# Two-layer cached attention with a token mixer: the K of the unit between the layers moved behind the last V of the unit at the change

## The chip, the cores and the metric

The kernel runs on one core of a Trainium2 chip. The metric is the device time of one execution in microseconds (us); the median of three runs is compared. In this text MB is a million bytes and GB/s a billion bytes a second.

## The reference

Two kinds of layer alternate, twice each: attention over a long cache for one new token, and a mixer.

```
h = layernorm(x)                                   # x: (2, 1, 512)
q = h @ wq                                         # 32 query heads of 128, 8 K/V heads
s = q . k_cache / sqrt(128)                        # 2 x 8 K/V heads, 32768 keys of 128 each
x = x + (softmax(s) . v_cache) @ wo
h = layernorm(x)
x = x + w2 . gelu(w1 * h + b1) + b2                # per channel, 1792 hidden values
```

All data are f32. One cache (K or V of one batch row and one head) is 16.8 MB, and there are 32 of them, read once in each of the two layers: some 1,061 MB cross the DMA queue, and this is nearly all the kernel does.

## The kernel before, in words

**Units.** The work is cut into 32 units (layer, batch row, K/V head). A unit has 8 chunks of K and 8 of V, 2.10 MB each (a `[128, 4096]` f32 tile). A K chunk takes 8 products on TensorE (line L481, 512 keys each; the trace counts each product as two MATMUL rows, so a chunk is x16), a V chunk likewise (L638). When all 8 K chunks of a unit are through, `max_1`, `max_2`, `turn_scores` and `exponentials` make the weights of its softmax, in two halves `S[0]` and `S[1]` of four chunks, and only then can its V chunks be multiplied. So the V of a unit comes after the K of the next one, normally.

**The units around the changes of layer.** Batch row 0 goes over to the second layer while batch row 1 is still in the first. With the numbers of the code: unit 12 is (layer 0, row 0, head 5), unit 13 = `N1` is (0, 0, 7) and ends row 0's first layer, unit 14 is (0, 1, 5), the unit "between the layers", and unit 15 is (1, 0, 7), the first of the second layer. The same happens for row 1 with units 16 = `N2`, 17 and 18. After the last V of unit 13 comes row 0's mixer (`mix_1`, `take_rows`, `mix_2`, `hidden_sum` with 14 hidden tiles, `mix_3`, `to_columns`), and from that the query of unit 15 (`q_products`, `make_q`).

**Memory.** SBUF holds 13.6 cells of one chunk each; loads go to cells 0 to 10, the other places hold weights. Head 7 is used by both layers in neighbouring units, so part of its K and V stays: K chunks 0, 1, 2 in cells 0, 1, 2 (`KEPT_K`) and V chunks 1, 2, 3, 5, 6, 7 and most of 4 (`KEPT`; chunk 4 lies in cell 13 and in the first part of cell 6). Between unit 13's V and unit 15's V only cells 6 and 7 are free for everything that passes; there the loads are half chunks (`[128, 2048]`, 1.05 MB), which rotate through the four half cells.

**Order.** Everything is planned in Python before the first instruction: `stream` is the list of loads, sorted by a key, and counts time in chunks; `at(time, f, ...)` books every other step at such a time (`kend`, `vend`: the chunk times when the unit's K and V are through); a load's cell is picked by `spread`, which takes the cell with the best `fit`. All cache loads are issued by one engine (SyncE, line L189) in the stream's order, through one queue. A load waits until the old contents of its cell have been used, and everything behind it waits too.

**The fold.** After unit 12 its result rows are added to x: `out_2` (4 products into `rows`, line L296), then `fold_rows`, which copies `rows` to cell 13 (DVE, L710) and turns it there (TensorE, L699). Both are booked at `vend + 2` of unit 12, two chunks after its last V. The load of unit 13's V chunk 4 into cell 13 has to wait for that.

```
    def fold_rows():
        y = mem[:, (WCELL0 + WCELLS) * CK :][:, :D]
        nc.vector.tensor_copy(y, rows)
        fold(y, 0, B)
```

Of the kernel before, what the change touches and what calls it, by code (L numbers as in the profile page):

```python
# [41 lines left out]
DIRECT = 2  # L42
TAIL_GROUPS = (3, 3, 3, 2, 1)
IDLE = (4, 1, 3, 2)
KEEP_UP = 3
EPS = 1e-5


@with_exitstack
def gqa_mixer_kernel(ctx: ExitStack, tc: tile.TileContext, x, kt, v, wqo, cols, out):  # L50
# [21 lines left out]
    NCH = kt.shape[1] // (CK * DH)  # L72
# [5 lines left out]
    NU = LAYERS * U  # L78
    NT = NCH * JT
    HALVES = NCH // PACK  # L80
# [24 lines left out]
    WCELL0, WCELLS = RING * RING, 4  # L105
# [129 lines left out]
    booked, closed = {}, {}  # L235
# [110 lines left out]
    def row_tile():  # L346

        return S[HALVES - 1]
# [450 lines left out]
    def last_mixer(n):  # L799
# [21 lines left out]
        for k in range(2):  # L821
# [14 lines left out]
        for g in range(NG):  # L836
# [7 lines left out]
            )  # L844
        idle_products(IDLE[1])

# [99 lines left out]
    def parts(n, with_v):  # L946

        m = n + with_v
        if m < N1 or n > N3 and m > N3 + 1:

            loads = ((0, 4), (4, 2), (6, 2)) if m == NU else ((0, 2), (2, 2), (4, 2), (6, 2)) if m == N3 + 2 else GROUPS
            return [(c, k, NCH) for c, k in loads]
        if not with_v:
            loads = ((0, 3), (3, 1), (4, 2), (6, 2)) if n in (N1, N2) else ((0, 2), (2, 2), (4, 2), (6, 2))
            if n in (N1 + 1, N2 + 1):
                loads = ((0, 2), *((c, 1) for c in range(2, NCH)))
            if n in (N1 + 2, N3):
                loads = [(c, 1) for c in range(NCH)]
        elif n in (N1, N2):
            loads = ((0, 1), (1, 3), (4, 1), (5, 2), (7, 1))  # L960
        elif n in (N1 + 1, N2 + 1):
            loads = [(c, 1) for c in range(NCH)]
        elif n < N1:
            loads = ((0, 2), (2, 2), (4, 2), (6, 2))
        else:
            loads = [(c, 1) for c in range(NCH)]
        return [(c, k, RING) for c, k in loads]

    stream = []
    for n in range(NU):  # L970
        stream += [(n * NCH + c + m - 1, 0, n, c, m, limit) for c, m, limit in parts(n, 0)]
        for i, (c, m, limit) in enumerate(parts(n, 1)):
            if n in (N1, N2):
                key = (n + 1) * NCH + 1 + (i + 1) / (2 * NCH)
            elif n in (N1 + 1, N2 + 1):
                key = (n + 1) * NCH - 0.5 + max(c / (2 * NCH) - 0.5, c - 2 + m)
            elif n - N1 in FOLLOWS:
                key = (n + 1) * NCH + FOLLOWS[n - N1][c]
            else:
                key = (n + 1) * NCH + c + m - 1 + (LAG if N1 - 1 <= n <= N3 else 0)  # L980
            stream.append((key, 1, n, c, m, limit))
# [3 lines left out]
    kbeg, k_done, vbeg, v_done, vend_of, v_from, v_to, brings, starts, t = {}, {}, {}, {}, {}, {}, {}, [], [], 0  # L985
# [13 lines left out]
    def at(time, f, *a, rank=1):  # L999
        done.setdefault(time, []).append((rank, f, a))  # L1000
# [3 lines left out]
    mixed = {}  # L1004
    for n in range(NU):
        layer, b, h = unit_of(n)
        kend, vend = k_done[n, NCH - 1], vend_of[n]
        ahead = vend_of[n - 1] if n else 0
        urgent = n in (N1, N2, NU - 1)
        if n:  # L1010
            if n in (N1 + 2, N2 + 2):
                q2 = mixed[layer - 1, b] + 0.5
                q3 = q2 + 1
                place = S[1]
            else:
                place = S[0] if n in (N2 + 1, N3 + 1) else None
                q0 = kbeg[n] - (10 if n == N3 + 1 else 4 if n == N3 + 2 else 6)
                q1, q2, q3 = q0 + 1, q0 + 2, q0 + 2
            assert q3 <= kbeg[n]
            if n not in (N1 + 2, N2 + 2):  # L1020
                apart = not N1 <= n <= N3 + 2 and h not in opens
                if apart and layer == 1:
                    at(kbeg[n] - 11, make_q, n, 4)
                    at(q0, make_q, n, 5)
                    at(q1, make_q, n, 6)
                else:
                    at(kbeg[n] - (11 if apart else 9) if apart or n == N1 - 1 else q0, make_q, n, 0)
# [15 lines left out]
        if n in (N1 + 1, N2 + 1):  # L1043
            for k in range(2, 2 * (NCH - 3)):
                at(kend - 0.5 * k - 0.5, idle_products, KEEP_UP, rank=3)
            at(kend - 0.5, turn_scores, n, 0, rank=2)
            at(kend, q_products, n + 1, 0)
            at(kend, max_1, n)
            at(kend, max_2, n)
            at(kend, q_products, n + 1, 1)  # L1050
            for k in range(HALVES):
                at(kend, exponentials_at_once, n, 0, k, HALVES)
            at(kend + 0.5, q_products, n + 1, 2, 3)
            t1 = kend + 2
            assert mixed[units[n - 1][:2]] == kend == kbeg[n + 1] - 2
            at(t1, turn_scores, n, 1, rank=2)
            at(t1, exponentials_at_once, n, 1, rank=2)
            at(t1 + 1, sums, n)
            assert t1 + 1 < v_done[n, HC] - 1
        else:  # L1060
            t1 = max(kend + 2, ahead + (2 if urgent else 4))
            e = kend if N1 < n <= N3 else kend + 2
            soon = n in (N1 + 2, N3)
            assert not soon or e == kend and vbeg[n] == kend
            at(max(kend, e - 1), max_1, n, rank=int(not soon))
            at(e, max_2, n, rank=int(not soon))
            t0 = max(k_done[n, HC - 1], *(v_done[n - 1, c] for c in range(HC) if n), 0)
            if n in (N2, N3):
                t0 = max(t0, kbeg[n + 1] - (7 if n == N3 else 3))
            at(t0, turn_scores, n, 0)  # L1070
            if soon:
                assert t0 < e and v_from[n] % HALVES == 1
                for k in range(HALVES):
                    at(e, exponentials_at_once, n, 0, HALVES - 1 - k, HALVES, rank=0)
                at(e + 1, sums, n, 1)
            else:
                at(e, exponentials, n, 0)
            if n == NU - 1:
                t1 = ahead
                assert t1 >= kend + 2 and vbeg[n] == ahead  # L1080
            at(t1, turn_scores, n, 1)
            at(t1, exponentials, n, 1)
        at(t1 + (1 if n == NU - 1 else 2), denominators, n)
        if n == NU - 1:
# [2 lines left out]
            at(vend, last_out, n)  # L1087
            at(vend, last_mixer, n)
            continue
        assert vbeg[n + 1] >= vend and (n + 2 >= NU or vbeg[n + 1] > vend)  # L1090
        change = n in (N1, N2)
        at(vend if change else min(vend + 1, vbeg[n + 1]), out_0, n)
        at(vend + 0.5 if change else min(vend + 1, vbeg[n + 1]), out_1, n)
# [6 lines left out]
            at(vend + 2, fold_rows)  # L1100
        if units[n] == lay[layer, b][-1]:
            key = (layer, b)
            at(vend - 1 if change else vend, mix_1, key)
            at(vend + (1 if change else 2), take_rows, key, row_tile())
            at(vend + (1.5 if change else 3), mix_2, key)
            at(vend + (0 if change else 1), gelu_table)
            if change:

                assert k_done[n + 1, NCH - 1] == vend + 6
                at(vend + 1.5, hidden_sum, key)  # L1110
                at(vend + 4.5, highest, n + 1, 0)
# [32 lines left out]
    first = next(t for t, (*_, n, _, m, limit) in zip(starts, stream) if n > N3 and m == PACK)  # L1144
    for k in range(0, NCH, PACK):
        book(k, 2 * PACK, first + k)
    closed[WCELL0] = closed[WCELL0 + 1] = kbeg[N2 + 1]
    closed[WCELL0 - 1] = kbeg[N3 + 2] - 8
    first_input()
    for step in range(4):  # L1150
# [90 lines left out]
```

## Time and profile before

| | |
|---|---|
| device time, three runs | 2488.03, 2488.17 (median), 2489.24 us |
| span of the profiled execution, first to last instruction | 2486.6 us |
| what the median has around that span | 1.6 us |
| TensorE busy | 1413.2 us, 57% |
| packets of the load queue | 99.2% of the time of 16 DMA engines |
| mean granted TensorE clock | 0.777 |

The profiled execution's device time is not listed apart from the three runs; its span is what the rows below are counted in, and the 1.6 us is taken as constant. A row of the chain or of the timeline gives start, duration, engine, line, and what was written from what; "idle before" tells what ended the wait. A row of the windows gives, for a stretch of time, the busy time of PE, PEld, DVE, ACT and POOL, then the granted clock, the DMA engines' busy share and the GB/s moved.

### The profile page before, as it was taken

To read this page: it belongs to the slowest core of one execution; us is meant where nothing else is said; L and a number is where in the kernel's file an instruction comes from. 1 tells how busy PE (TensorE), PEld (TensorE's weight loads), DVE (VectorE), ACT (ScalarE), POOL (GpSimd) and SP (SyncE) were. 2 spreads that over 40 slices of the span, in tenths; PEclk is the share of its full clock that TensorE was granted. 3 is DMA by queue.
4 is the path that set the end of the run, shared out by engine and by line. 5 is a ranking of instruction groups with operands and counts; after the bars stand their busy time and mean duration, and the time that the engine had idled before them with its cause. 6 is when DMAs were issued, how large, how long until landed. Compare 5 with 4: busy or idle time off the path is not lost.

```text
span 2486.6 us, 20856 instructions
## 1 busy us (share of the span) xinstructions
PE 1413.2 (57%) x9438; PEld 386.1 (16%) x9438; DVE 256.6 (10%) x659; ACT 185.5 (7%) x544; POOL 4.9 (0%) x17
## 2 busy tenths in 40 slices
PE   4544545556555454657677675455555664456546
PEld 1111111111111111112122121111111111111112
DVE  1000000000000000003113110000000000010002
ACT  0000000000000000002012000000000000011002
POOL 0000000000000000000000000000000000000000
PEclk8777777776777777888888887777677777777878
DMA  9999999999999999999999999999999999999996
GB/s 421 434 433 429 433 437 430 434 436 431 427 435 431 436 427 432 431 429 412 431 433 415 429 432 432 434 435 430 436 429 429 429 435 434 428 436 431 434 435 287
DMA packets 30594, 1062.54 MB, mean 427 GB/s; under 512 B 3749, under 2 KB 3753, under 8 KB 4394
## 3 DMA queue, kind: packets, MB, share of 16 engines
q1 hardware_dynamic: 30216, 1061.17, 99.2%
q8 instruction: 74, 1.21, 0.2%
q14 instruction: 14, 0.11, 0.0%
q10 hardware_dynamic: 290, 0.04, 0.0%
HBM read 1061.19 MB, written 0.00 MB: 427 GB/s over the span
## 4 chain that ended last, share of the span: by engine, by line
DMA 72%; PE 26%; DVE 0%; issue 0%; another core or an unknown queue 0%; ACT 0%; SPq 0%; ACTq 0%
DMA mem<-in_v_dram 61%; PE acc L638 20%; DMA mem<-in_kt_dram 10%; PE scores L481 3%; DMA mem<-in_wqo_dram 2%; PE kept L162 1%; PE kept L395 1%; PE small L669 0%; PE small L510 0%; PE bcast L395 0%; PE small L797 0%; PE small L504 0%; PE kept L296 0%; PE kept L849 0%
## 5 line engine op out<-in xcount | busy, mean ns | idle before, releaser
L481 PE MATMUL scores<-mem,small_sb 128*32 128x512 f32 x4096 | 615.7, 724 | 544.5 <-DMA mem<-in_kt_dram 544.4
L638 PE MATMUL acc<-mem,S 128*16 128x512 f32 x4088 | 621.3, 737 | 473.0 <-DMA mem<-in_v_dram 471.3
L481 PEld LDWEIGHTS scores<-mem,small_sb 128*32 128x32 f32 x4096 | 147.2, 127 | 914.6 <-issue 839.2
L521 ACT ACTIVATE S<-S,small_sb 128x128 f32<-128x128 f32 x232 | 119.3, 518 | 1974.6 <-DVE small_sb L512 1377.0
L638 PEld LDWEIGHTS acc<-mem,S 128*16 128x16 f32 x4088 | 132.6, 110 | 839.6 <-issue 699.1
L496 DVE TENSOR_REDUCE small_sb<-scores 128x1 f32<-128x512 f32 x64 | 44.3, 692 | 743.8 <-PE scores L481 743.8
L516 DVE STREAM_TRANSPOSE S<-scores 128x512 f32<-128x512 f32 x64 | 45.5, 710 | 141.4 <-PE acc L638 137.2
L395 PE MATMUL kept<-mem,small_sb 128*2 128x512 f32 x96 | 54.5, 691 | 3.9 <-DMA mem<-in_wqo_dram 2.1
L296 PE MATMUL kept<-mem,small_sb 128*1 128x512 f32 (+1 forms) x236 | 42.1, 597 | 2.7 <-ACT mem L892 2.4
L521 ACT ACTIVATION_READ_ACCUMULATOR S<-S,small_sb 128x1 f32 x232 | 43.3, 187 | 0.0
L506 DVE TENSOR_REDUCE small_sb<-small 1x4 f32<-1x128 f32 x32 | 8.9, 279 | 294.1 <-PE small L504 294.1
L671 DVE RECIPROCAL small_sb<-small 128x4 f32<-128x4 f32 x32 | 5.9, 185 | 321.6 <-PE small L669 321.6
L680 DVE TENSOR_TENSOR small_sb<-small,small_sb 128x4 f32<-128x4 f32 x31 | 5.1, 164 | 299.1 <-PE small L678 299.1
L608 DVE SCALAR_TENSOR_TENSOR S<-acc,small_sb,S 128x128 f32<-128x128 f32 x93 | 32.6, 351 | 3.3
L892 ACT ACTIVATE S<-bcast,small_sb 128x512 f32<-128x512 f32 x28 | 21.6, 778 | 89.9 <-DVE small_sb L761 87.8
L606 DVE TENSOR_SCALAR S<-acc,small_sb 128x128 f32<-128x128 f32 x31 | 10.8, 350 | 146.7 <-PE acc L638 146.7
L162 PE MATMUL kept<-mem,small_sb 48*2 48x512 f32 x32 | 25.2, 929 | 0.0
L421 PE MATMUL small<-small_sb,mem 2*128 2x2 f32 x112 | 14.7, 248 | 17.9 <-DVE mem L417 17.9
L395 PE MATMUL bcast<-mem,small_sb 128*1 128x512 f32 (+1 forms) x40 | 20.9, 640 | 0.0
L678 PEld LDWEIGHTS small<-small_sb,S 128*128 128x128 f32 x62 | 13.2, 266 | 48.7 <-issue 41.9
L797 PE MATMUL small<-small_sb 128*128 128x128 f32 x120 | 18.7, 290 | 0.0
L504 PE MATMUL small<-small_sb 128*1 128x128 f32 x64 | 16.7, 354 | 3.3 <-DVE small_sb L502 3.3
(154 smaller groups left out, 340.9 us busy)
## 6 DMA issues: line engine op xcount, KB each, us to landing
mem<-in_kt_dram SPq DMA_DIRECT2D x14, 4096.0 KB
mem<-in_v_dram SPq DMA_DIRECT2D x11, 4096.0 KB
mem<-in_v_dram SPq DMA_DIRECT2D x13, 2048.0 KB
mem<-in_kt_dram SPq DMA_DIRECT2D x12, 2048.0 KB
mem<-in_kt_dram SPq DMA_DIRECT2D x24, 1024.0 KB
mem<-in_v_dram SPq DMA_DIRECT2D x21, 1024.0 KB
mem<-in_wqo_dram SPq DMA_DIRECT2D x4, 3840.0 KB
mem<-in_wqo_dram SPq DMA_DIRECT2D x3, 4096.0 KB
```

What stands on the lines that cost most here:

```text
L162: nc.tensor.matmul(q_ps[n][:B, :], low[:, j * B : (j + 1) * B], lowered[h][:, j * D : (j + 1) * D], start=(j == 0), stop=False,)
L296: nc.tensor.matmul((rows if to is None else to)[32 * g : 32 * g + b + 1, :], weights if b else weights[:, 1:], row, start=to is not None, ...
L395: nc.tensor.matmul(q_ps[n][:m, :], xnT[:, d, b : b + m], wq_at(h, d), start=(d == 0 and h not in lowered), stop=(d == last),)
L481: nc.tensor.matmul(sc_ps[n, half][32 * g : 32 * g + 32, :], q, kc[k * NG + g], start=(i == 0 and k == 0), stop=(i == PACK - 1 and k == SUB ...
L496: nc.vector.tensor_reduce(mx[n][:, half : half + 1], sc_ps[n, half], axis=AX.X, op=ALU.max)
L504: nc.tensor.matmul(pm[:1, :P], mxa, ident, start=True, stop=True)
L516: nc.vector.transpose(S[half], sc_ps[n, half])
L521: nc.scalar.activation(s[:, :, h], s[:, :, h], AF.Exp, bias=neg[n][:, h : h + 1], scale=SCALE, accum_out=lsum[n][:, half, h : h + 1],)
L608: nc.vector.scalar_tensor_tensor(t, acc[:, k * DH : (k + 1) * DH], mask[:, k : k + 1], t, op0=ALU.mult, op1=ALU.add)
L638: nc.tensor.matmul(acc[32 * g : 32 * g + R * QT, :], S[half][:, col : col + R * QT], vc[q], start=(c == v_from[n] and q < NG), stop=(c == ...
L797: nc.tensor.matmul(p[:, :P], ident, ident, start=True, stop=True)
L892: nc.scalar.activation(hid[key, f], px[key], AF.Gelu_apprx_tanh, bias=shift[key][:, f : f + 1], scale=slope[key][:, f : f + 1],)
```

## The change

Three keys of `stream` and the steps booked by them are changed, at both changes of layer (units 13 to 15 and 16 to 18):

- The first two K chunks of unit 14 came as one load ahead of unit 13's V. Now all eight come behind unit 13's last V, each as two half chunks.
- Unit 15's K chunks 0 and 1, which are resident, are now multiplied before unit 14's first V, and not among its V chunks; unit 15's query is made two chunks of K earlier than the end of unit 14's K. Unit 14's softmax steps move behind that.
- V chunks 5 and 6 of unit 13 are two loads, not one. V chunks 2, 3 and 4 of unit 14 are now loaded whole and no longer in halves.
- `idle_products` (10 products on data that nobody reads) are added around the last two V chunks of unit 13.
- Unit 12's `out_2` and `fold_rows` keep their times, `vend + 2`. Unit 13's softmax is booked earlier by one or two chunks.

```
+BETWEEN = (1.1, 1.2, 1.3, 2.1, 2.2, 3.1, 4.1, 5.1)
...
             if n in (N1 + 1, N2 + 1):
-                loads = ((0, 2), *((c, 1) for c in range(2, NCH)))
+                loads = [(c, 1) for c in range(NCH)]
...
         elif n in (N1, N2):
-            loads = ((0, 1), (1, 3), (4, 1), (5, 2), (7, 1))
+            loads = ((0, 1), (1, 3), (4, 1), (5, 1), (6, 1), (7, 1))
...
-        stream += [(n * NCH + c + m - 1, 0, n, c, m, limit) for c, m, limit in parts(n, 0)]
+        late = 0.5 if n in (N1 + 1, N2 + 1) else 0
+        stream += [(n * NCH + c + m - 1 + late, 0, n, c, m, limit) for c, m, limit in parts(n, 0)]
...
             if n in (N1, N2):
-                key = (n + 1) * NCH + 1 + (i + 1) / (2 * NCH)
+                key = (n + 1) * NCH + (i + 1) / (2 * NCH)
             elif n in (N1 + 1, N2 + 1):
-                key = (n + 1) * NCH - 0.5 + max(c / (2 * NCH) - 0.5, c - 2 + m)
+                key = (n + 1) * NCH + BETWEEN[c]
...
+                if n in (N1 + 1, N2 + 1):
+                    q0 = k_done[n - 1, NCH - 1] - 6
...
-            at(kend, q_products, n + 1, 0)
-            at(kend, max_1, n)
-            at(kend, max_2, n)
-            at(kend, q_products, n + 1, 1)
+            at(kend + 0.5, max_1, n)
+            at(kend + 1, max_2, n)
             for k in range(HALVES):
-                at(kend, exponentials_at_once, n, 0, k, HALVES)
-            at(kend + 0.5, q_products, n + 1, 2, 3)
+                at(kend + 1, exponentials_at_once, n, 0, k, HALVES)
...
-            t1 = max(kend + 2, ahead + (2 if urgent else 4))
-            e = kend if N1 < n <= N3 else kend + 2
+            t1 = max(kend + 2, ahead + (0 if n == N1 else 2 if urgent else 4))
+            e = kend if N1 < n <= N3 else kend + (1 if n == N1 else 2)
...
-        assert vbeg[n + 1] >= vend and (n + 2 >= NU or vbeg[n + 1] > vend)
+        assert vbeg[n + 1] >= vend and (n + 2 >= NU or vbeg[n + 1] > vend or n == N1 - 1)
...
-            at(vend - 1 if change else vend, mix_1, key)
+            at(vend - 2 if change else vend, mix_1, key)
+            if change:
+                for k in (2, 1):
+                    at(vend - k, idle_products, BEFORE, rank=2)
...
-                assert k_done[n + 1, NCH - 1] == vend + 6
+                assert k_done[n + 1, NCH - 1] == vend + 8
...
-    closed[WCELL0] = closed[WCELL0 + 1] = kbeg[N2 + 1]
+    closed[WCELL0] = closed[WCELL0 + 1] = k_done[N2, NCH - 1]
```

The load queue at the first change (SyncE), from the last V of unit 12 on. The width 2048 is a half chunk, 4096 a chunk, 12288 three chunks, 2560 and 1536 the two parts of unit 13's V chunk 4; the brackets name the semaphores waited for. Before:

```order
L189 DMA mem<-in_v_dram 128x8192 [waits DMAHW3_49,PE_49]
L189 DMA mem<-in_kt_dram 128x8192 [waits DMAHW5_49,DMAHW0_49,PE_49]
L189 DMA mem<-in_v_dram 128x4096 [waits DMAHW6_49,PE_49]
L189 DMA mem<-in_v_dram 128x12288 [waits DMAHW4_49,PE_49]
L189 DMA mem<-in_v_dram 128x2560 [waits DVE_49,PE_49,Pool_49]
L189 DMA mem<-in_v_dram 128x1536 [waits DMAHW7_49]
```

and with the change:

```order
L191 DMA mem<-in_v_dram 128x8192 [waits DMAHW5_49,PE_49]
L191 DMA mem<-in_v_dram 128x4096 [waits DMAHW0_49]
L191 DMA mem<-in_v_dram 128x12288 [waits DMAHW4_49,DMAHW2_49]
L191 DMA mem<-in_v_dram 128x2560 [waits DVE_49,PE_49,Pool_49]
L191 DMA mem<-in_v_dram 128x1536 [waits DMAHW6_49]
```

The 4.19 MB of unit 14's first K are gone from between unit 12's and unit 13's V. The load that waits for DVE and PE (width 2560) goes to cell 13 and stands directly behind the three-chunk load in both. In the built program its DVE wait is for the copy of `fold_rows` and its PE wait for the fold's last product. The cells differ, too: unit 13's last K load goes to cells 5 and 6 (7 and 8 before) and unit 12's last V load to cells 3 and 4 (5 and 6 before), so that the latter waits for V chunks 4 and 5 of unit 12 where it waited for chunks 2 and 3.

TensorE at the same place, from unit 13's last two K chunks on (`scores_2360` is unit 13's score tile, `scores_2440` unit 14's, `S0` and `S1` the weights, `kept2` the tile `rows`). Before:

```order
L481 MATMUL scores_2360<-mem_68,small_sb_66 32x512 x16
L638 MATMUL acc_83<-mem_68,S1_91 16x512 x8
L504 MATMUL small_92<-small_sb_66 1x128
L638 MATMUL acc_83<-mem_68,S1_91 16x512 x8
L510 MATMUL small_92<-small_sb_66 128x4
L481 MATMUL scores_2440<-mem_68,small_sb_66 32x512 x8
L678 MATMUL small_92<-small_sb_66,S1_91 128x4
L481 MATMUL scores_2440<-mem_68,small_sb_66 32x512 x8
L296 MATMUL kept2_87<-mem_68,small_sb_66 1x512 x4
L699 MATMUL small_92<-small_sb_66,mem_68 128x2 x4
L638 MATMUL acc_83<-mem_68,S0_90 16x512 x16
```

and with the change:

```order
L483 MATMUL scores_2360<-mem_68,small_sb_66 32x512 x16
L506 MATMUL small_92<-small_sb_66 1x128
L640 MATMUL acc_83<-mem_68,S1_91 16x512 x8
L512 MATMUL small_92<-small_sb_66 128x4
L640 MATMUL acc_83<-mem_68,S1_91 16x512 x8
L680 MATMUL small_92<-small_sb_66,S1_91 128x4
L640 MATMUL acc_83<-mem_68,S0_90 16x512 x16
L298 MATMUL kept2_87<-mem_68,small_sb_66 1x512 x4
L701 MATMUL small_92<-small_sb_66,mem_68 128x2 x4
```

The fold (kept2, then the small products of L699, now L701) stood behind unit 14's first two K chunks and ahead of unit 13's V. Now unit 13's V chunks 0 and 1 (the x16 on `S0`) stand ahead of it, and chunk 1 is part of the three-chunk load.

TensorE at the end of unit 14's K (`scores_2638` before, `scores_2652` now), where unit 15's scores begin (`scores_2749`, now `scores_2731`). Before:

```order
L481 MATMUL scores_2638<-mem_68,small_sb_66 32x512 x4
L395 MATMUL bcast_88<-mem_68,small_sb_66 1x512
L504 MATMUL small_92<-small_sb_66 1x128
L510 MATMUL small_92<-small_sb_66 128x4
L395 MATMUL bcast_88<-mem_68,small_sb_66 1x512
L638 MATMUL acc_83<-mem_68,S0_90 16x512 x4
```

and with the change:

```order
L483 MATMUL scores_2652<-mem_68,small_sb_66 32x512 x4
L483 MATMUL scores_2731<-mem_68,small_sb_66 32x512 x4
L506 MATMUL small_92<-small_sb_66 1x128
L483 MATMUL scores_2731<-mem_68,small_sb_66 32x512 x4
L512 MATMUL small_92<-small_sb_66 128x4
L483 MATMUL scores_2731<-mem_68,small_sb_66 32x512 x8
L640 MATMUL acc_83<-mem_68,S0_90 16x512 x16
```

The maximum of unit 14's scores (L504, L510) had the products of unit 15's query (bcast) between its steps; now it has unit 15's two resident chunks, 16 products, between the last K and the first V.

More of the change, by code (lines that the diff above doesn't have):

```diff
@@ L44 @@
 IDLE = (4, 1, 3, 2)
+BETWEEN = (1.1, 1.2, 1.3, 2.1, 2.2, 3.1, 4.1, 5.1)
 KEEP_UP = 3
+BEFORE = 5
 EPS = 1e-5
@@ L1045, in gqa_mixer_kernel @@
                 at(kend - 0.5 * k - 0.5, idle_products, KEEP_UP, rank=3)
+            q = mixed[units[n - 1][:2]]
+            assert q + 2 == kend == kbeg[n + 1]
+            at(q, q_products, n + 1, 0, 1)
+            at(q + 0.5, q_products, n + 1, 2, 3)
             at(kend - 0.5, turn_scores, n, 0, rank=2)
-            at(kend, q_products, n + 1, 0)
-            at(kend, max_1, n)
-            at(kend, max_2, n)
-            at(kend, q_products, n + 1, 1)
+            at(kend + 0.5, max_1, n)
+            at(kend + 1, max_2, n)
             for k in range(HALVES):
-                at(kend, exponentials_at_once, n, 0, k, HALVES)
-            at(kend + 0.5, q_products, n + 1, 2, 3)
+                at(kend + 1, exponentials_at_once, n, 0, k, HALVES)
             t1 = kend + 2
-            assert mixed[units[n - 1][:2]] == kend == kbeg[n + 1] - 2
             at(t1, turn_scores, n, 1, rank=2)
@@ L1068, in gqa_mixer_kernel @@
             if n in (N2, N3):
-                t0 = max(t0, kbeg[n + 1] - (7 if n == N3 else 3))
+                t0 = max(t0, kbeg[n + 1] - 7 if n == N3 else kend - 3)
             at(t0, turn_scores, n, 0)
```

## The prediction, made before the changed kernel was run

> **What bounds the kernel now.** I read the page first, for what is busy all the time.
>
> ```profile
> span 2486.6 us, 20856 instructions
> PE 1413.2 (57%) x9438; PEld 386.1 (16%) x9438; DVE 256.6 (10%) x659; ACT 185.5 (7%) x544; POOL 4.9 (0%) x17
> ...
> DMA  9999999999999999999999999999999999999996
> GB/s 421 434 433 429 433 437 430 434 436 431 427 435 431 436 427 432 431 429 412 431 433 415 429 432 432 434 435 430 436 429 429 429 435 434 428 436 431 434 435 287
> ...
> q1 hardware_dynamic: 30216, 1061.17, 99.2%
> ```
>
> The load queue never rests: its packets fill 99.2% of the span on all 16 DMA engines, while TensorE is busy for 57%. So the time is the bytes over the rate, plus every moment in which the queue is dry. TensorE's work counts only where it makes the queue dry, by keeping a cell from the next load. Apart from the first and the last, the only slices under 420 are 412 and 415, and those hold the two changes of layer (a slice is 62.2 us: 1119 to 1181 and 1306 to 1368). The windows there, cut where the load of unit 13's (16's) V ends and where the half chunks of the next unit's K end:
>
> ```profile
> 1100.00:1139.50 39.50, 21.61 (x144) 5.81 (x148) 5.16 (x13) 5.74 (x18) 0.00 (x0) 0.78 1.00 429
> 1139.50:1170.70 31.20, 28.33 (x201) 11.33 (x194) 15.61 (x28) 12.87 (x17) 0.54 (x1) 0.95 0.99 401
> 1170.70:1195.80 25.10, 20.74 (x157) 5.99 (x156) 8.23 (x20) 1.38 (x3) 0.54 (x1) 1.00 1.01 421
> ...
> 1327.90:1358.10 30.20, 26.58 (x194) 10.76 (x186) 15.24 (x28) 12.87 (x17) 0.54 (x1) 0.96 1.01 415
> 1358.10:1383.20 25.10, 21.39 (x166) 6.43 (x158) 8.47 (x20) 1.38 (x3) 0.54 (x1) 1.00 1.02 422
> ```
>
> The last column is GB/s. With half chunks and nothing late the queue moves 421 to 422, with larger pieces 429. Against 421, the stretch of unit 14's K at 401 lost (1 - 401/421) x 31.2 = 1.5 us, and the second one (1 - 415/422) x 30.2 = 0.5 us. These 2.0 us are all that the change can win at these places; the whole kernel has little else to give.
>
> **The first change of layer: the fold.** What can be lost is seen in the waits of the load queue's engine and in the chain at the same place.
>
> ```profile
> SPq L189 <- PE small L699: 23.1, 1, 23.1
> ```
> ```profile
> 1073.94 5.36 PE acc L638 x32
> ...
> 1079.32 23.64 DMA mem<-in_kt_dram
> ...
> 1103.09 3.64 PE scores L481 x16
> 1106.73 0.52 PE small L678 x2
> 1107.25 2.39 PE scores L481 x16
> 1109.64 0.91 PE kept L296 x8
> 1110.55 0.02 issue
> 1110.58 0.70 DVE mem L710
> 1111.28 0.04 issue
> 1111.33 1.07 PE small L699 x8
> ...
> 1112.44 0.33 SPq L189
> ```
>
> For 23.1 us the issuing engine stands at one load, that of unit 13's V chunk 4 into cell 13, until the fold is out of that cell. Nothing is issued meanwhile. In the kernel before this costs nothing: TensorE can do the fold once unit 14's first K chunks have landed (1103.09), and behind them the queue still holds unit 13's V chunks 0 to 3, 8.4 MB. The fold is done at 1112.4, and the three-chunk load is used only from 1122.45:
>
> ```profile
> 1083.56 5.34 PE L481 MATMUL scores<-mem,small_sb 128*32 128x512 f32 x32 [4.30 <-DMA mem<-in_kt_dram]
> ...
> 1122.45 3.34 PE L638 MATMUL acc<-mem,S 128*16 128x512 f32 x16 [8.24 <-DMA mem<-in_v_dram]
> ...
> 1144.38 1.91 PE L638 MATMUL acc<-mem,S 128*16 128x512 f32 x16
> ```
>
> In the order of the changed kernel TensorE has unit 13's V chunks 0 and 1 ahead of the fold, and chunk 1 is the first of the three-chunk load, which has one completion. So the fold waits for the whole of that load; and the load for cell 13, the next in the queue, waits for the fold. Behind the three-chunk load nothing is issued. The queue must run dry there, and stays so for the sum of
>
> - TensorE's chunk 1 after an idle wait: 3.34 us, the same instructions at 1122.45 in the kernel before, which also come cold out of a wait (warm they take 1.91, which I keep as the lower end);
> - `out_2`, the copy, the turning, the issue: from 1109.64 to 1112.44, 2.80 us;
> - the fixed time F of a load on an empty queue, from issue to first use beyond its bytes.
>
> F stands in no single row, so I bound it.
>
> ```profile
> 0.74 0.39 SPq L129 DMA_DIRECT2D mem<-in_wqo_dram  x1
> ...
> 32.50 7.76 PE L481 MATMUL scores<-mem,small_sb 128*32 128x512 f32 x52 [7.12 <-DMA mem<-in_kt_dram]
> ```
> ```profile
> 1368.11 6.82 DMA mem<-in_v_dram
> 1374.92 0.04 issue
> 1374.97 1.05 PE acc L638 x8
> ```
>
> At the kernel's start two loads, 4.19 and 8.39 MB, go out at 0.74 and are used at 32.50; at 429 GB/s 12.58 MB take 29.3, which leaves 2.4 us. In the stretch of half chunks a load went from issue to use in 6.82 us; its own 1.05 MB take 2.5 at 421, and part of the other 4.3 was a queue that still held something. So F is 2.4 to 4.3. I take 4.3: it is the row from the middle of the same stream, where the 16 DMA engines do not run in step, while the start has them all idle together. The dry time is then 3.34 + 2.80 + 4.3 = **10.4 us**; with the low ends, 1.91 + 2.80 + 2.4 = 7.1. The Trainium skill ("DMA: Bandwidth & Descriptors", the section on the anatomy of one DMA) puts the fixed cost of one DMA at about 2.0 us, fitted on DMAs that GpSimd issues; by that figure the dry time would be an estimated 8.1 and the total 2.3 us less than mine. The trace, with 2.4 at its lowest, lies a little above it.
>
> **The other edits.**
>
> - *Unit 12's last V load* now waits for TensorE's V chunks 4 and 5 (cells 3 and 4), and is issued at 1079.3, when the row at 1073.94 ends; in the queue ahead of it is only the end of unit 13's last K, used from 1083.56. That is 4.24 us from issue to use, against F = 4.3: 0.1 us dry, at most 0.1 by these bounds, and nothing if F is smaller. The two loads behind it wait for nothing late.
> - *Unit 14's K*: its first four half chunks are now in the queue before unit 13's V is finished, as before four others were; but unit 13's chunks 5, 6 and 7 are three loads, so when the last lands TensorE has one chunk left and not three. In the kernel before, two chunks (6.25 us for the pair at the low clock) and then the last chunk's 1.91 stood there. I count the 2.0 us as won.
> - *Sizes of pieces*: per change, 4.19 MB go from large pieces to half chunks (at 421 instead of 429, +0.2 us), 6.29 MB from half chunks to whole ones (-0.3). Both changes together: -0.2.
> - *Mixer, query and unit 14's softmax*: the mixer's work is the same. Its length against the eight chunks of K behind which it must hide is read from these rows.
>
> ```profile
> 1146.36 0.35 DVE L606 TENSOR_SCALAR S<-acc,small_sb 128x128 f32<-128x128 f32 x1 [17.10 <-PE acc L638]
> ...
> 1168.29 1.12 PE L917 MATMUL bcast<-S,small_sb 128*128 128x512 f32 x2 [0.36 <-DVE S L909]
> ...
> 1182.44 0.16 DVE L429 COPY small_sb<-small 128x4 f32<-128x4 f32 x1 [2.77 <-PE small L421]
> ```
>
> From `out_0` to `mix_3` it takes 21.9 us, to the ready query 36.2 (with unit 14's softmax steps in between). Sixteen half chunks take 16 x 2.5 = 40 us, so the query is there when unit 15's resident chunks are due, with some 4 us over. Those chunks, 2 x 1.9 us of products, hide the maximum and the exponentials of unit 14, which in the kernel before had the query's products. The loads that wait for them still have at least one or two half chunks ahead. I cost this at nothing; if the cover is gone, each change loses what the query is late.
> - *The extra idle products* lie in TensorE's waits for V chunks 6 and 7: nothing. Unit 13's softmax is booked earlier, and TensorE needs nothing of it that isn't due long before the three-chunk load has landed: nothing.
> - *The second change of layer* has no fold: `fold_rows` is called once, after unit 12. The load into cell 13 there finds a free place, and the queue holds over 20 MB worth of issued or issuable loads behind it. Nothing is lost.
>
> **The sum**, in the span: +10.4 + 0.1 - 2.0 - 0.2 = **+8.3**, so 2494.9; with the 1.6 us that the median has around this span, **2496.5 us**, or 0.33% slower. What can be told from no change is 0.2%, or 5.0 us: 2483.2 to 2493.1.
>
> **The rivals.**
>
> *The dry queue doesn't come, and only the gain stays.* It ends on the other side, if TensorE's chunk 1 needs to wait only for its own third of the three-chunk load. Then it starts two chunks, 4.19 MB or 9.8 us, earlier, 0.6 of the 10.4 us stay, and the sum is +0.6 + 0.1 - 2.2 = -1.5: 2486.7 us. For it: in the kernel before the same 23.1 us wait is free. Against it: the row at 1122.45 shows TensorE waiting 8.24 us for this load, and only then going through chunks 1, 2 and 3. It decides where the fold's wait ends: 10 us before the three-chunk load has landed it would be free.
>
> *The fixed time and the cold clock are at their low ends*: 7.1 - 2.2 = +4.9, or 2493.1. This is the lower edge of the first case, at which slower turns into no change.
>
> *The K of unit 14 runs into a new wait.* Its 16 half chunks have four half cells, and TensorE must take each within the three that are in flight, some 7 us. If the mixer's query is late for the resident chunks, the V loads behind wait in both changes. For it: 4 us are all that is over, on a chain of 36. Against it: the order puts unit 15's query before the last half chunk of K, and the kernel before shows the same chain with its interruptions. A query 4 us later than reckoned, at both places, less the half chunk ahead in the queue, loses 2 x 2 = 4 us: 2500.5.
>
> **How the numbers follow.** Dry queue at the fold, as summed: 82 in 100, with a range of 2493 to 2498.5. No dry queue: 9. Dry queue and a late query: 9. Of the first case I give 1 in 100 to a time under 2493.1, so slower is 81 + 9 = 90; of the second, 2 go to faster by over 0.2% and 7 to no change, with the 1 from the first 8. The range takes in the first case with its low edge and the third: 2493 to 2501.
>
> **What would show it.** In the waits of the load queue's engine, the wait for the fold (now L701) is near 38 us instead of 23.1. At about 1112.8 (1122.45 less 9.8 us for the 4.19 MB that no longer stand ahead, plus 0.1) TensorE starts on the three-chunk load, at about 1118.9 the next load is issued, and the slice of the GB/s row that holds it falls from 429 to about 360. The stretch of unit 14's K, shifted, runs at 420 or more, not at 401, and at the second change there is no hole. If the slices show no hole, the fold's wait was free after all and the first rival holds; if the hole is there and the time is not 8 us longer, the gain was more than the 2.0 us that the windows show; and if a second hole stands at the end of unit 14's K, the query was late.

## The result, and the profile after

| | before | changed |
|---|---|---|
| median | 2488.10 us (2488.03 to 2489.24, 5 runs) | 2502.21 us (2500.00 to 2503.54, 5 runs) |
| ratio | | 1.0054, 95% interval 1.0043 to 1.0065 |
| span of the profiled execution | 2486.6 us | 2501.7 us |

The changed kernel is 14.1 us slower. The prediction said 8.3 us and a range that ended at 2501.0, so it is out of its range by 1.2 us, on the slow side. The profiled execution of the changed kernel is the slowest of its five (2503.54 us). Lines of the changed kernel stand two higher than before: the loads at L191, the products of K at L483 and of V at L640, the fold at L298, L712 and L701.

From the page of the changed kernel:

```profile
GB/s 420 435 433 428 437 434 433 431 433 431 434 434 428 434 435 432 424 348 418 427 423 415 424 429 432 432 433 433 434 430 431 435 431 432 432 434 434 427 434 283
...
q1 hardware_dynamic: 30504, 1061.17, 98.7%
```

The bytes are the same, the queue's share is half a per cent lower, and one slice has fallen: the 18th, 1063 to 1126 us, from 429 to 348. The two slices under 420 of before are still there as 418 and 415.

The waits of the load queue's engine, in the changed kernel:

```profile
SPq L191 <- PE small L701: 39.5, 1, 39.5
```

and its chain around the fold (start, duration, what):

```profile
1079.72 32.73 DMA mem<-in_v_dram
...
1112.50 3.62 PE acc L640 x16
1116.11 1.70 PE kept L298 x8
...
1117.84 0.70 DVE mem L712
...
1118.58 1.07 PE small L701 x8
...
1119.70 0.33 SPq L191
```

TensorE gets the three-chunk load at 1112.50 and the fold only behind it; the next load goes out at 1119.70. What the queue does meanwhile is in the windows of the changed kernel (columns as before: busy time of PE, PEld, DVE, ACT, POOL, granted clock, DMA share, GB/s):

```profile
1110.00:1120.00 10.00, 6.35 (x33) 1.79 (x33) 0.93 (x3) 0.00 (x0) 0.00 (x0) 0.62 0.01 5
1113.00:1118.00 5.00, 4.76 (x24) 0.64 (x16) 0.16 (x1) 0.00 (x0) 0.00 (x0) 0.54 0.00 0
...
1109.50:1112.00 2.50, 0.00 (x0) 0.00 (x0) 0.00 (x0) 0.00 (x0) 0.00 (x0) 0.50 0.28 118
1112.00:1120.50 8.50, 6.85 (x38) 2.18 (x42) 1.04 (x4) 0.00 (x0) 0.00 (x0) 0.67 0.00 0
```

From 1110 to 1120 the queue moves 5 GB/s. This is the hole that the prediction placed here. The last two rows give its size without any other run: the 16 DMA engines do not end the three-chunk load together (0.28 of them are busy on average from 1109.5 to 1112.0), and then nothing moves for 8.5 us, so (1 - 0.28) x 2.5 + 8.5 = 10.3 us of the queue are lost. By the packet records the first packets of the next load start at 1120.66, 0.96 us after its issue.

There is a second place. The chain of the changed kernel at the end of unit 14's K:

```profile
1167.90 1.07 PE scores L483 x8
...
1170.69 1.00 PE scores L483 x8
...
1174.11 1.00 PE scores L483 x8
1175.10 1.70 PE bcast L397 x4
1176.80 0.86 PE small L799 x6
1177.67 1.00 PE scores L483 x8
1178.66 1.70 PE bcast L397 x4
1180.36 0.86 PE small L799 x6
1181.22 1.85 PE scores L483 x16
1183.08 0.98 PE small L423 x8
1184.06 2.03 PE scores L483 x16
...
1189.46 2.62 PE acc L640 x24
...
1192.10 17.80 DMA mem<-in_v_dram
```

and its windows:

```profile
1175.00:1180.00 5.00, 5.00 (x26) 1.41 (x21) 0.00 (x0) 0.00 (x0) 0.00 (x0) 1.00 1.02 419
1180.00:1185.00 5.00, 5.00 (x39) 2.29 (x39) 1.46 (x3) 0.00 (x0) 0.00 (x0) 1.00 0.98 369
1185.00:1190.00 5.00, 5.00 (x48) 1.57 (x48) 3.42 (x9) 0.75 (x2) 0.00 (x0) 1.00 0.98 390
1190.00:1195.00 5.00, 3.40 (x30) 0.78 (x22) 2.36 (x4) 0.63 (x1) 0.00 (x0) 1.00 1.02 365
```

From 1167.90 to 1192.08 the chain runs through TensorE, with only a short step on DVE in it (0.5 us, from 1172.68), and no wait for a transfer; TensorE is busy in 5.00 of 5.00 us from 1175 to 1190 while the queue goes from 419 to 369 and 390, and it moves 365 in the window after that. The rows say why. For each of the last two of four half chunks TensorE has its scores (1.00), two products of unit 15's query (1.70) and a group of idle products (L799, 0.86), 3.56 us together; the first two take 2.79 and 3.42, with the end of the mixer (L919, L366) in place of the query. From the scores at 1167.90 to those at 1181.22 four half chunks take 13.3 us, and the queue brings four in 10 (2.5 us each). Behind that come the scores of the last three half chunks, the turning of the query (L423) and the two resident chunks, before the first V of unit 14 is touched. The half cells come free late, and so the loads are issued late. The DMA share stays near 0.98, so engines hardly stand still; it is packets that are longer. Those of 8 KB took 0.31 us from 1165 to 1175, and some that started from 1183.2 to 1183.4, about 1 us behind the load issued at 1182.28, took up to 1.23 us. In the kernel before, the chain waits for transfers at the same place:

```profile
1163.02 8.77 DMA mem<-in_kt_dram
...
1171.84 1.11 PE scores L481 x8
```

At the second change the same piece of chain runs from 1346.88 to 1378.81 without a wait for a transfer.

### The profile page after: what moved, and what is told of

It reads as the page before. It is cut to its first block, busy times and chain, and to the rows that moved or that the text cites. A ratio compares the mean times of both kernels' runs of the same rounds, so it can differ in the third digit from the quotient of the medians.

```text
span 2501.7 us, 20938 instructions
## 1 busy us (share of the span) xinstructions
PE 1425.7 (57%) x9478; PEld 393.0 (16%) x9478; DVE 256.5 (10%) x659; ACT 185.5 (7%) x544; POOL 4.9 (0%) x17
## 4 chain that ended last, share of the span: by engine, by line
DMA 72%; PE 26%; issue 0%; another core or an unknown queue 0%; DVE 0%; ACT 0%; SPq 0%; ACTq 0%
DMA mem<-in_v_dram 60%; PE acc L640 19%; DMA mem<-in_kt_dram 11%; PE scores L483 3%; DMA mem<-in_wqo_dram 2%; PE kept L164 1%; PE kept L397 1%; PE small L799 1%; PE small L512 0%; PE small L671 0%; PE bcast L397 0%; PE kept L298 0%; SPq L191 0%; PE small L506 0%
## 5 line engine op out<-in xcount | busy, mean ns | idle before, releaser
L483 PE MATMUL scores<-mem,small_sb 128*32 128x512 f32 x4096 | 618.5, 725 | 549.1 <-DMA mem<-in_kt_dram 549.1
L640 PE MATMUL acc<-mem,S 128*16 128x512 f32 x4088 | 617.3, 736 | 469.5 <-DMA mem<-in_v_dram 465.9
L483 PEld LDWEIGHTS scores<-mem,small_sb 128*32 128x32 f32 x4096 | 147.3, 127 | 922.5 <-issue 838.4
L640 PEld LDWEIGHTS acc<-mem,S 128*16 128x16 f32 x4088 | 131.2, 109 | 829.2 <-issue 693.3
L298 PE MATMUL kept<-mem,small_sb 128*1 128x512 f32 (+1 forms) x236 | 43.1, 612 | 2.7 <-ACT mem L894 2.4
L799 PE MATMUL small<-small_sb 128*128 128x128 f32 x160 | 25.1, 297 | 1.0 <-DVE small_sb L371 1.0
L423 PE MATMUL small<-small_sb,mem 2*128 2x2 f32 x112 | 14.7, 249 | 17.9 <-DVE mem L419 17.9
L799 PEld LDWEIGHTS small<-small_sb 128*128 128x128 f32 x160 | 21.0, 199 | 16.6 <-issue 15.4
```

Source lines behind the costliest of these rows:

```text
L298: nc.tensor.matmul((rows if to is None else to)[32 * g : 32 * g + b + 1, :], weights if b else weights[:, 1:], row, start=to is not None, ...
L423: nc.tensor.matmul(pt[:, r * m : (r + 1) * m], q_row[n][:m, r * DH : (r + 1) * DH], ident[:m, :m], start=True, stop=True,)
L483: nc.tensor.matmul(sc_ps[n, half][32 * g : 32 * g + 32, :], q, kc[k * NG + g], start=(i == 0 and k == 0), stop=(i == PACK - 1 and k == SUB ...
L640: nc.tensor.matmul(acc[32 * g : 32 * g + R * QT, :], S[half][:, col : col + R * QT], vc[q], start=(c == v_from[n] and q < NG), stop=(c == ...
L799: nc.tensor.matmul(p[:, :P], ident, ident, start=True, stop=True)
```

## The experiments

The first four ran beside runs of the kernel before with a median of 2488.63 us, the next four beside 2488.31, the last two beside 2488.28.

**1. The changed kernel with the early fold.** Unit 12's `out_2` and `fold_rows` are booked at `vend`, ahead of unit 13's first V chunk.

```
-            at(vend + 1 if change else vend if n == NU - 2 else vend + 2, out_2, n, acc if change else None)
+            at(vend + 1 if change else vend if n in (NU - 2, N1 - 1) else vend + 2, out_2, n, acc if change else None)
...
-            at(vend + 2, fold_rows)
+            at(vend, fold_rows)
```

> The changed kernel with one thing moved: unit 12's out_2 and fold_rows stand ahead of unit 13's V chunks 0 and 1, not behind them. Theory (the fold holds the load queue): the hole of some 10 us at 1112 to 1122 us goes, the issuing engine's wait for the fold falls under 25 us, and the time falls by 9 to 10.5 us, to about 2492. Rival (the time is lost to the new pieces and their order, and the hole only shows where it is paid): the hole reappears elsewhere and the time stays above 2498.

Measured: 2491.65 us (2490.14 to 2493.99), ratio 1.0011 (1.0002 to 1.0021). That is 10.6 us under the changed kernel. Its waits and its chain:

```profile
SPq L191 <- PE small L701: 23.7, 1, 23.7
```
```profile
1104.20 0.33 SPq L191
```

The wait is as long as in the kernel before (23.1) and as free. So the fold's place carries 10.6 of the 14.1 us, and 3.0 us over the kernel before are left for something else.

**2. The kernel before with the late fold, and nothing else of the change.**

```
-            at(vend + 1 if change else vend if n == NU - 2 else vend + 2, out_2, n, acc if change else None)
+            at(vend + 1 if change else vend if n == NU - 2 else vend + (4 if n == N1 - 1 else 2), out_2, n, acc if change else None)
...
-            at(vend + 2, fold_rows)
+            at(vend + 4, fold_rows)
```

> The kernel before with one thing moved: out_2 and fold_rows of unit 12 stand two chunks later, behind unit 13's V chunks 0 and 1, and nothing else is changed. Theory: the same hole of 9 to 11 us comes behind the three-chunk load, and the time is 2497 to 2499. Rival (the hole needs the K that was moved out of the way): it is a few us at most, under 2491, since unit 14's first K still stands ahead.

Measured: 2498.69 us (2498.09 to 2500.13), ratio 1.0039 (1.0024 to 1.0054), 10.1 us over the runs beside it. The wait and the chain:

```profile
SPq L189 <- PE small L699: 38.8, 1, 38.8
```
```profile
1122.53 3.62 PE acc L638 x16
1126.14 1.19 PE kept L296 x8
...
1129.23 0.33 SPq L189
```

The same hole, made in the kernel before by this one edit. That unit 14's K stands elsewhere isn't needed for it; what counts is that the fold stands behind the first use of the three-chunk load.

**3. The changed kernel with the three-chunk load cut in two**, so that unit 13's V chunk 1 has a completion of its own. The late fold stays. (With it, the planner puts unit 12's last V load into other cells.)

```
-            loads = ((0, 1), (1, 3), (4, 1), (5, 1), (6, 1), (7, 1))
+            loads = ((0, 1), (1, 1), (2, 2), (4, 1), (5, 1), (6, 1), (7, 1)) if n == N1 else ((0, 1), (1, 3), (4, 1), (5, 1), (6, 1), (7, 1))
```

> The changed kernel with unit 13's V chunks 1 to 3 as two loads, chunk 1 alone and chunks 2 and 3 together; the fold stays behind chunk 1. Theory (the fold waits for the completion of the load that holds chunk 1): the fold can be done 9.8 us of queue time earlier, the hole shrinks from about 10 us to 0 to 1, and the time is about 2492 to 2493. Rival (the hole is the fold's own length): it stays near 6 us, 2498.

Measured: 2491.88 us (2490.37 to 2495.25), ratio 1.0014 (1.0004 to 1.0024); 10.3 us under the changed kernel, with this wait:

```profile
SPq L191 <- PE small L701: 7.9, 1, 7.9
```

The fold comes after the same products as in the changed kernel, and the hole is gone. So the hole is made by the one completion for three chunks: the first rival's condition (chunk 1 need wait only for its own third) is right as a condition, it just isn't met by a load of three chunks.

**4. The early fold and fewer idle products**: of the eight groups along the last half chunks of unit 14's and unit 17's K, the four nearest the end are left out.

```
-            for k in range(2, 2 * (NCH - 3)):
+            for k in range(6, 2 * (NCH - 3)):
                 at(kend - 0.5 * k - 0.5, idle_products, KEEP_UP, rank=3)
```

> As the kernel with the fold ahead of unit 13's V, and without the 12 idle products behind the last four half chunks of K of units 14 and 17 (they write nothing that is read). Theory (at the end of that K TensorE, with two query products and three idle products per half chunk, needs 3.6 us for each where the queue brings one every 2.5, and so becomes the bound): without them a half chunk takes 2.7 us, and 2 to 3 us go at both places together, to about 2489 to 2490. Rival (the loss there comes from the resident chunks alone, which hold the cells): under 1 us, 2491 to 2492. Second rival (the clock falls without the idle products): slower than with them.

Measured: 2488.88 us (2488.03 to 2490.90), ratio 1.0001 (0.9992 to 1.0011): 2.8 us under experiment 1, and the kernel before again. Its chain waits for transfers at the end of unit 14's K, as before, and its windows there show no dip:

```profile
1160.98 8.77 DMA mem<-in_kt_dram
...
1169.80 1.11 PE scores L483 x8
...
1170.93 9.74 DMA mem<-in_v_dram
```
```profile
1170.00:1175.00 5.00, 4.42 (x42) 1.73 (x34) 1.86 (x5) 0.00 (x0) 0.00 (x0) 1.00 1.01 416
1175.00:1180.00 5.00, 4.47 (x39) 1.18 (x34) 4.04 (x8) 1.39 (x3) 0.00 (x0) 1.00 1.03 424
```

This also tells a busy TensorE from a late query, which was the third rival: the query's products are all still there, at their places, and the loss is gone. Only part of the time taken out comes back: four groups are 3.3 us of TensorE a change (0.67 + 0.94 + 0.86 + 0.86), the gain is 1.4 us a change, and then TensorE waits for transfers again.

**5. The early fold, fewer idle products, and unit 13's last K load in cells 7 and 8 as before**, so that unit 12's last V load needn't wait for its V chunks 4 and 5.

```
-            bufs = spread(m, until, n in (N1 + 1, N2 + 1) and m == 1)
+            bufs = spread(m, until, n in (N1 + 1, N2 + 1) and m == 1, 7 if (n, c) == (N1, 6) else None)
```

> As the kernel with the early fold and without the last 12 idle products, and unit 13's last K load put back into cells 7 and 8, so that unit 12's last V load goes out when V chunks 2 and 3 are used and not only after chunks 4 and 5. Theory (the late issue leaves the queue short at 1079 to 1092 us): the 1.0 to 1.5 us lost there come back, to about 2487.5 (ratio to the kernel before 0.999 to 1.000). Rival (the queue was short but not dry): no change, 2488.9.

Measured: 2489.54 us (2488.01 to 2491.17), ratio 1.0005 (0.9996 to 1.0014). Nothing is gained over experiment 4. The late load is real: by the packet records, the first 465 MB have crossed 0.9 us later in the changed kernel and in experiment 4 than before, and in experiment 5 at the same time. But at 500 MB, some 80 us later, both experiments are within 0.1 us of the kernel before. So no loss from the late load can be told in the time.

**6. The kernel before, with unit 13's and 16's V chunks 5 and 6 as two loads, and nothing else of the change.**

```
-            loads = ((0, 1), (1, 3), (4, 1), (5, 2), (7, 1))
+            loads = ((0, 1), (1, 3), (4, 1), (5, 1), (6, 1), (7, 1))
```

> The kernel before with one part of the change: V chunks 5 and 6 of units 13 and 16 as two loads. Theory (the low rate at 1140 to 1160 comes from TensorE having three chunks of V left when the last V lands, since the pair lands as one): the rate there rises from about 400 to 415 or more and the time falls by 0.8 to 1.5 us, to about 2487. Rival (the low rate is the mixer's start and the small loads): no change in the rate.

Measured: 2488.43 us (2488.04 to 2490.03), ratio 1.0001 (0.9992 to 1.0010): no change. In its windows the rate at unit 14's K moves, and nothing comes of it:

```profile
1139.50:1170.70 31.20, 25.76 (x176) 10.31 (x174) 16.02 (x30) 12.86 (x17) 0.56 (x2) 0.95 0.99 410
1170.70:1195.80 25.10, 21.67 (x151) 6.12 (x155) 7.56 (x17) 1.39 (x3) 0.53 (x1) 0.93 1.01 410
```

Over both windows these are 410 GB/s, and in the kernel before (401 x 31.2 + 421 x 25.1) / 56.3 = 410 too.

**7. Experiment 5 without any of these idle products.**

```
-            for k in range(2, 2 * (NCH - 3)):
+            for k in ():
```

> As the kernel with the early fold and the old cells, with none of the idle products that run along the K of units 14 and 17 (they write nothing that is read). Theory (TensorE's time there is what counts, and the products cost more than the clock that they keep): no loss against the kernel with some of them, 2487 to 2488.5. Rival (without them the granted clock falls and the scores and query products take up to 1.8 times as long): the queue runs short again at the end of that K and the time is 2 to 5 us longer.

Measured: 2488.92 us (2488.25 to 2490.75), ratio 1.0003 (0.9994 to 1.0012). The window at unit 14's K:

```profile
1139.50:1170.70 31.20, 24.88 (x135) 5.30 (x127) 15.63 (x28) 12.87 (x17) 1.09 (x2) 0.82 1.01 415
```

The granted clock there falls to 0.82, where the kernel before has 0.95 and experiment 5 has 0.89, and the time doesn't move.

**8. Experiment 1 with the four groups nearest the end of K doubled** instead of left out.

```
-                at(kend - 0.5 * k - 0.5, idle_products, KEEP_UP, rank=3)
+                at(kend - 0.5 * k - 0.5, idle_products, 2 * KEEP_UP if k < 6 else KEEP_UP, rank=3)
```

> The changed kernel with the early fold, with twice as many idle products (6 in place of 3) behind each of the last four half chunks of K of units 14 and 17. Theory (TensorE is the bound there, with no wait between 1169 and 1192 us): 12 products of 0.29 us more at each place, 3.4 us each, come back in full, 6 to 7 us in all, to about 2498. Rival (the loss there is the resident chunks' holding of the cells): under 2 us, 2492 to 2493.

Measured: 2496.84 us (2495.40 to 2497.61), ratio 1.0033 (1.0021 to 1.0045), 5.2 us over experiment 1. Its chain stays on TensorE from 1147.39 to 1184.51, and its windows at the end of K sink further:

```profile
1172.12 1.53 PE small L799 x12
```
```profile
1170.00:1175.00 5.00, 5.00 (x36) 2.08 (x31) 0.68 (x1) 0.00 (x0) 0.00 (x0) 1.00 0.74 274
1175.00:1180.00 5.00, 5.00 (x48) 1.97 (x42) 1.91 (x5) 0.00 (x0) 0.00 (x0) 1.00 0.84 324
```

Twelve more idle products a change make each of the four groups 0.67 us longer (1.53 for 0.86 in the row above), 2.7 us of TensorE, and cost 2.6 us a change: here all of it is paid. (The expectation had reckoned 3.4 us, by the length of a whole group of three.) With experiment 4 this shows TensorE as the bound there: less work on it gives time back, more work takes time.

**9. The changed kernel with fewer idle products as in experiment 4, and its late fold.**

> The changed kernel with its late fold, and four of the eight groups of idle products at the end of unit 14's and unit 17's K left out (products nobody reads). My theory: the dry queue at the fold (10.5 us by the early fold) and the busy TensorE at the ends of K (2.8 us by fewer idle products, with the early fold) lie at different places and add up, so this lands 2.8 us under the changed kernel: 2499.4, 2498.4 to 2500.4. The rival: with the late fold everything behind runs 10 us later with fewer loads in flight, and the idle products cost something else there: under 1 us saved (2501.2 or more) or over 4 us (2498 or less).

Measured: 2499.16 us (2498.63 to 2501.41), ratio 1.0043 (1.0028 to 1.0058), 3.1 us under the changed kernel. With and without the hole at the fold, the idle products cost 3.1 and 2.8 us: the two losses add up.

**10. The kernel before without the idle products along unit 14's and unit 17's K.**

> The kernel before, with the idle products along unit 14's and unit 17's K left out altogether (products nobody reads). Two theories of the 401 GB/s in unit 14's K in the kernel before. Mine: that rate is not made by TensorE, since with the changed order and less idle the windows there rise to 420 and fall by as much in 1100 to 1139.5 (429 to 419), the sum over 1060 to 1450 staying at 425 GB/s; so no change, 2487.8 to 2488.8, and 425 over that stretch. The rival: the idle products hold TensorE back there as they do in the changed kernel, and without them the kernel gains the 1.5 us that the window at 401 shows: 2486.8 or less, with 410 or more in the window 1139.5 to 1170.7 and 427 over the stretch.

Measured: 2488.41 us (2487.91 to 2489.16), ratio 0.9999 (0.9990 to 1.0008). Its windows:

```profile
1139.50:1170.70 31.20, 22.52 (x156) 5.50 (x148) 16.01 (x30) 12.86 (x17) 0.67 (x2) 0.92 0.99 409
1170.70:1195.80 25.10, 21.71 (x154) 6.09 (x154) 7.72 (x17) 1.38 (x3) 0.41 (x1) 0.93 1.01 412
```

409 and 412 instead of 401 and 421, and no time: as in experiment 6, rate goes from the second window to the first. In the kernel before the idle products lie in TensorE's waits and cost nothing; in the changed order they don't.

None of these versions is faster than the kernel before by more than the measurement can tell.

## Why the prediction was wrong, step by step

**The fold: right.** The wait was to be near 38 us and is 39.5; TensorE was to start on the three-chunk load at 1112.8 and did at 1112.50; the next load was to go out at 1118.9 and did at 1119.70; the slice was to fall to about 360 and fell to 348. The term was 10.4 us, and the fold's place is worth 10.6 (experiment 1) and 10.1 (experiment 2). That the whole came out this close is luck in part, since two of its parts were off and nearly cancel. From the wait's end to the issue it took 7.25 us, not 6.14: `out_2` took 1.70 us, where I took 0.91 from the kernel before. There it came out of a busy TensorE; here TensorE had idled 9.90 us, and the granted clock in the window 1113 to 1118 is 0.54. The Trainium skill ("TensorE: Matmul & The Clock Gate", part 1, on the clock gate) says that the array is clocked at half rate after an idle window and needs about 3.4 us of sustained work, in a window that runs freely, to get the full clock. The trace agrees: the work is slow from 1112.50 until `out_2` ends at 1117.81, 5.3 us; in experiment 2, out of a like wait, `out_2` took 1.19 us, so the slow stretch has no fixed length here. That leaves 10.6 - 7.25 = 3.3 us or, by experiment 2, 10.1 less 6.7 (1122.53 to 1129.23) = 3.4 us for the fixed time F, inside my 2.4 to 4.3 and a microsecond below the 4.3 that I took. (These are differences of medians whose runs scatter by a microsecond and more; the 10.3 us of the windows less the same 7.25 give 3.1.) Of it 1.8 us are the engines that run out one after the other, (1 - 0.28) x 2.5, and 1.0 is the time from the issue to the first packets.

**"I cost this at nothing", of the mixer, the query and unit 14's softmax: wrong.** This is the step that put the time out of the range: with four groups of idle products fewer, and all else as in the change, it is 2499.16 us (experiment 9), inside. I looked only at whether the query's chain fits into 40 us of K. I didn't add up what TensorE has to do in the last half chunks of unit 14's K in the new order. The groups of idle products along K were there before, and harmless; the change brought unit 15's query products and the resident chunks forward into the same half chunks. Then 13.3 us of TensorE's time stand against 10 us of transfer, ahead of two resident chunks. Four of the groups cost 2.8 us (experiment 4) to 3.1 us (experiment 9) over both changes. The idle products that the change adds around unit 13's last V are others; I costed them at nothing too, and that stands, since experiment 4 keeps them and runs in the time of the kernel before. My third rival named the place and gave 2500.5, but its mechanism, a late query, isn't it: from 1167.90 to 1192.08 TensorE stands still for 0.5 us, on a step of DVE.

**The gain of 2.0 us: not there.** I read the 401 in the window of unit 14's K as time that the change could win. It won the rate there, and not the time. Windows over more of the stream, before and in experiment 4:

```profile
1060.00:1139.50 79.50, 43.93 (x276) 11.55 (x280) 6.68 (x19) 5.74 (x18) 0.00 (x0) 0.78 1.00 429
1146.00:1148.00 2.00, 1.22 (x13) 0.20 (x5) 1.40 (x4) 0.00 (x0) 0.00 (x0) 1.00 0.76 315
...
1060.00:1450.00 390.00, 273.76 (x1848) 79.68 (x1852) 81.03 (x178) 45.67 (x96) 2.17 (x4) 0.86 1.01 425
```
```profile
1078.00:1080.25 2.25, 1.42 (x12) 0.13 (x4) 0.00 (x0) 0.00 (x0) 0.00 (x0) 0.96 0.81 350
...
1060.00:1139.50 79.50, 48.94 (x334) 14.86 (x334) 8.73 (x25) 5.79 (x18) 0.00 (x0) 0.83 0.99 423
1139.50:1170.70 31.20, 25.66 (x148) 8.39 (x148) 15.58 (x28) 12.86 (x17) 1.09 (x2) 0.89 1.01 420
...
1060.00:1450.00 390.00, 276.39 (x1852) 79.28 (x1856) 81.96 (x179) 45.71 (x96) 2.17 (x4) 0.86 1.01 425
```

With the reordering freed of its two costs, 401 has become 420 as predicted, and the window ahead of it has gone from 429 to 423; the 415 of the second change is still 415 in experiment 4. Over both changes the queue moves 425 GB/s either way, and the ratio of the times is 1.0001. Three orders with three splits of the rate, those of experiments 4, 6 and 10, give one time. At least part of the dip before is a load issued late: the next one goes out only at 1147.21, and from 1146 to 1148 a quarter of the DMA engines stands idle (share 0.76, some 0.5 us of the queue), with packets of up to 1.6 us behind it. Experiment 4 has 0.97 there, but 0.81 from 1078 to 1080.25, behind unit 12's late V load, some 0.4 us. Experiment 5 has 0.99 and 1.02 in these two windows, and it is no faster. Why closing these gaps moves the rate and not the time is not settled; that the half chunks and the pieces of unit 13's V chunk 4 are transfers slower than the rest would fit, but was not tried alone.

**The small terms.** Unit 12's late V load (+0.1) put the stream 0.9 us behind and cost nothing that could be measured (experiment 5). The sizes of pieces (-0.2) are too small to be seen.

**The sum.** 10.6 for the fold and 2.8 to 3.1 for the busy TensorE are 13.4 to 13.7 of the 14.1 us; the remaining half microsecond is less than can be told. Against the prediction's +8.3: 2.9 us for the term costed at nothing, 2.0 for the gain that didn't come, and some 0.9 in all the rest.

## What to carry to other kernels

In a kernel bound by one load queue, look for the load that waits for a compute step, and ask what that step now waits for: if it is a transfer of several pieces with one completion, and nothing is issued behind it, the queue runs dry for the whole chain from that completion to the issue, plus, in these runs, some 3 us. Here cutting the transfer was as good a cure as moving the step (10.3 and 10.6 us).

When work is moved on an engine that looks half idle, add up its rows for each transfer at the new place and hold the sum against that transfer's time; 57% busy over the kernel said nothing about four half chunks with 13.3 us of TensorE's time against 10 us of transfer. And before a dip in one window is counted as winnable, widen the window until it has the neighbours that may have taken the difference.

## What was not expected of the hardware

Products whose only purpose is to keep TensorE busy bought nothing here, and cost 2.8 us as soon as the real work left no room for them: without them the granted clock in the window of unit 14's K is 0.82 in the changed order (0.89 with four of the eight groups) and 0.92 in the order before (0.95 with all eight), with no effect on the time (experiments 7, 5 and 10). The Trainium skill ("Perfetto Trace Analysis", optimization strategies) says that in general the goal is to keep the matmul engine as busy as possible; in this stretch the trace goes the other way, since TensorE busy in 5.00 of 5.00 us stands beside the queue's 369 and 390 GB/s, and less work on it brings back 416 and 424.

A late load that put the stream 0.9 us behind at 465 MB left no trace in the time that could be told: 35 MB later this was made up. Of the hole of 10 us nothing was.
